# Writing the high half of each output row from ScalarE instead of VectorE, in an attention and two-stage MLP kernel

## The chip, the cores and the metric

The kernel runs on one core of a Trainium2 chip. Times are device microseconds (us) of one execution, from launch to end. Five engines work side by side, each on its own in-order queue: TensorE (PE: matmuls; PEld: its weight loads), VectorE (DVE), ScalarE (ACT), GpSimd (POOL) and SyncE (SP), the last of which issues most of the DMAs. Instructions of different engines wait for each other by semaphores.

## The reference

Three stages follow one another, all in float32:

```
scores = x @ state^T / 8;  a = softmax(scores);   xread = a @ state          # 8 x 8 heads, 512 rows, 32 states, 64 wide
scores2 = state @ x^T / 8; a2 = softmax(scores2); sread = a2 @ x
t = rows of [xread, sread], 4352 x 512
u = (sigmoid(t @ w_gate) * (t @ w_val)) @ w_out                              # 512 -> 1536 -> 512
e = argmax(u @ moe2_w_gate); p = softmax(u @ moe2_w_gate)[e]
out = p * (relu(u @ w1[e]) @ w2[e])                                          # 8 experts, 512 -> 1024 -> 512
```

The kernel does float32 products as three matmuls of float16 halves: every operand is scaled by a power of two and split into a high half (the value rounded to float16) and a low half (the scaled value minus the high half).

## The kernel before, in words

After a preparation, the function `token_block` runs for blocks b = 0 to 7, one for each batch of 512 tokens. A block has a gate phase and an output phase. In the gate phase `gate_val` is called for 12 feature chunks: matmuls L686 to L688, a sigmoid on ScalarE (L692), a product on VectorE (L694), the high half on ScalarE (L699) and the low half on GpSimd (L700). In the output phase `mlp_out` is called for four row tiles of 128 tokens: 36 matmuls (L744 to L746) sum into one PSUM buffer `po`. VectorE then takes the maximum of each row (L750), makes a power of two `s` of it in two tiny instructions (L142, L143), writes the high half of the scaled row as float16 into `xrow` (L755) and then the low half (L756). Two more row tiles, of the state rows, follow behind block 7: 34 row tiles in all. The rows are later sent by GpSimd to a table in DRAM, sorted by expert (`route`), and from about 780 us on the expert matmuls read them.

PSUM buffers of the kind `mm` number four. Gates, output tiles and the state weights share them.

Other work is woven into a block at marks. `mid()` is called twice in each gate chunk (marks 1 to 24) and three times in each output tile (marks 25 to 36: after the matmuls of feature chunks 3 and 7, and at the end of the tile, behind L756; the tile ends are marks 27, 30, 33 and 36). At a mark, fixed pieces are issued by number: the attention of the next block (`att_unit`, whose last piece, at marks 33 and 36, copies a result out of PSUM on ScalarE, L463), the state weights of the next block (`state_weights`, at marks 24, 26, ... 34: matmuls L489, high half on ScalarE L498, low half on VectorE L500), and the routing of this block (`route`: at mark 27 matmuls and a copy of the logits by ScalarE, L774; at mark 29 their transposes, L778). Behind these, `pump(bg)` takes one step of a background generator. From block 1 on this is `conv_experts`, which loads 64 chunks of expert weights and splits them, in three steps a chunk, one step a mark: (1) the high half on ScalarE and the low half on VectorE (L321, L322); (2) the bound of the next chunk, a sum of absolute values on ScalarE, two instructions on line L638; (3) the load of a later chunk, and the spread of the bound over the partitions by a tiny matmul (L202, reading the tile `em`), from which VectorE makes the scale. The pump runs at every output mark, and at the gate marks whose number is not a multiple of three.

The order of TensorE's instructions is as written (L960). The order on the other engines is made by a planner that simulates the program, gives precedence to what is written first, and keeps one kind of extra edge: under `tc.issue_after(ins)` the instructions of the block that run on the engine of `ins` are queued behind it. `mid()` opens such a block from block 1 on:

```
            for k in "AD":
                if k in last:
                    pins.enter_context(tc.issue_after(last[k].ins))
...
            with behind() if b else ExitStack():
                for f in todo.get(half[0], ()):
                    f()
```

`last["A"]` is an instruction of ScalarE and `last["D"]` one of VectorE. Before the change they are set by `gate_val` (L693, L694), by `state_weights` (L498, L500), and `last["D"]` also by `mlp_out` (L756).

Of the kernel before, what the change touches and what calls it, by code (L numbers as in the profile page):

```python
# [13 lines left out]
AF = mybir.ActivationFunctionType  # L14
ALU = mybir.AluOpType
# [11 lines left out]
def attention_moe_router_kernel(  # L27
# [24 lines left out]
    nc = tc.nc  # L52
    B, H, S, D = x.shape
    NS = state.shape[2]
    NT, DM = out.shape
# [77 lines left out]
    def tl(shape, dt=F32, name="t", bufs=None, pool=None):  # L133
        kw = {} if bufs is None else {"bufs": bufs}
        return (pool or tiny).tile(shape, dt, name=name, tag=name, **kw)

    def pow2_scale(m, k, nm, lim=40, inv=True, bufs=None, out=None, sh=0):

        n = m.shape[1]
        a = tl([P, n], I32, nm + "a")  # L140
        s = tl([P, n], I32, nm + "s", bufs) if out is None else out.bitcast(I32)
        nc.vector.tensor_scalar(a, m.bitcast(I32), EXPO, EXPO, ALU.bitwise_and, ALU.bitwise_xor)  # L142
        nc.vector.tensor_scalar(  # L143
            s, a, float((128 + lim) * ONE), float((k - 1) * ONE), ALU.min, ALU.add
        )
        if not inv:
            return s.bitcast(F32), None
        c = tl([P, n], I32, nm + "c", bufs)
        nc.vector.tensor_scalar(c, s, -1.0, float((254 - sh) * ONE), ALU.mult, ALU.add)
        return s.bitcast(F32), c.bitcast(F32)  # L150
# [42 lines left out]
    def mm_ps(shape):  # L193
        return mm_p.tile(shape, F32, name="mm", tag="mm")
# [22 lines left out]
    last = {}  # L217
# [520 lines left out]
    def mlp_out(t, j, acts, mid):  # L738

        po = mm_ps([P, DM])  # L740
        for fc, (h, lo) in enumerate(acts):
            hj, lj = h[:, j * P:(j + 1) * P], lo[:, j * P:(j + 1) * P]
            wh = wout[:, fc, 1] if t else ho[fc // 4][:, fc % 4]
            nc.tensor.matmul(po, hj, wh, start=(fc == 0), stop=False)  # L744
            nc.tensor.matmul(po, hj, wout[:, fc, 0], start=False, stop=False)  # L745
            nc.tensor.matmul(po, lj, wh, start=False, stop=(fc == NFC - 1))  # L746
            if fc in (3, 7):
                mid()
        m = tl([P, 1], name="xm")
        nc.vector.tensor_reduce(m, po, axis=AX.X, op=ALU.max, apply_absolute_value=True)  # L750
        r = rt[t // 4]
        s, _ = pow2_scale(m, 2, "xs", lim=80, inv=False, out=r["s"][:, j:j + 1])
        row = xrow[t % 4]
        pr = row[:, 0:DM].bitcast(F16)
        nc.vector.tensor_scalar(pr[:, 0:DM], po, s, None, ALU.mult)  # L755
        last["D"] = nc.vector.scalar_tensor_tensor(  # L756
            pr[:, DM:2 * DM], po, s, pr[:, 0:DM], op0=ALU.mult, op1=ALU.subtract
        )
        mid()
# [361 lines left out]
    def token_block(b):  # L1121
# [95 lines left out]
        for j in range(NJ):  # L1217
            mlp_out(NJ * b + j, j, acts, mid)
# [108 lines left out]
    for j in range(NST):  # L1327
        mlp_out(NXT + j, j, acts, lambda: next(tail, None) if j == 1 else None)
# [171 lines left out]
```

## Time and profile before

| | us |
|---|---|
| median of three runs | 1178.92 (1177.67 to 1181.25) |
| the profiled execution | 1176.91 |
| its span, from the first to the last instruction | 1175.2 |
| TensorE matmuls busy | 1077.7 (92%) |
| VectorE busy | 849.7 (72%) |
| ScalarE busy | 560.0 (48%) |
| GpSimd busy | 284.7 (24%) |
| L755, the instruction that is moved, 34 times | 25.5 |

The profile is of one execution. Busy time is the time in which an engine ran an instruction; the share is of the whole span, over stages with different limits. In the timeline a row gives start, duration, engine, line, operation, output and inputs, shapes and count; a bracket tells how long the engine had been idle before and what ended that. TensorE's clock has two levels, 1.2 and 2.4 GHz; a granted clock of 1.00 is the higher one all the time.

### The profile page before, as it was taken

The numbers are of one execution on the slowest core, as the hardware profiler recorded it, in microseconds if no ns is written. First come the engines' busy times: TensorE is split into PE (matmuls) and PEld (weight loads), VectorE is DVE, ScalarE is ACT, GpSimd is POOL, SyncE is SP. The second block draws the span as 40 slices with busy tenths as digits, with TensorE's granted clock in tenths as the row PEclk, the third lists the DMA queues.
The fourth block names the chain that finished last, engine by engine and source line by source line (L and its number), as shares of the span: only waits on it lengthen the run. The fifth ranks groups of instructions, "written<-read, shape, count | busy, mean of one in ns | idle before, by whom it ended". The sixth has DMA issues, their size and how long they took to land. (4 is left out here: it accounts for less than half of the span.)

```text
span 1175.2 us, 22595 instructions
## 1 busy us (share of the span) xinstructions
PE 1077.7 (92%) x8459; PEld 590.9 (50%) x8459; DVE 849.7 (72%) x2068; ACT 560.0 (48%) x970; POOL 284.7 (24%) x293
## 2 busy tenths in 40 slices
PE   3277689899999999998999999999999999999997
PEld 2122244444344444443444445866677666776664
DVE  7899966887887978878879756258666666665664
ACT  3676755757857768568577663311111111111111
POOL 1122211524415425134053250410000000000000
PEclk9978789999999999999999999999999999999999
DMA  7515492737657576476666451653222495989339
GB/s 259 193 58 163 113 178 61 221 103 226 183 160 227 148 204 203 113 202 193 162 210 169 143 196 55 207 182 129 57 56 56 144 358 124 281 288 363 60 103 280
DMA packets 187745, 200.66 MB, mean 171 GB/s; under 512 B 130159, under 2 KB 154735, under 8 KB 184304
## 3 DMA queue, kind: packets, MB, share of 16 engines
q1 hardware_dynamic: 172736, 147.51, 45.6%
q0 software_dynamic: 14896, 51.67, 11.5%
q8 instruction: 68, 1.11, 0.4%
q14 instruction: 45, 0.37, 0.1%
HBM read 217.40 MB, written 54.88 MB: 232 GB/s over the span
## 5 line engine op out<-in xcount | busy, mean ns | idle before, releaser
L935 ACT CAST acth<-v 128x256 f16<-128x256 f32 x148 | 60.1, 406 | 329.0 <-DVE v L934 306.0
L700 POOL TENSOR_TENSOR actl<-g,acth 128x512 f16<-128x512 f32 (+1 forms) x108 | 140.0, 1300 | 182.2 <-ACT acth L699 181.7
L688 PE MATMUL mm<-aT,M 128*128 128x512 f16 x384 | 149.6, 390 | 15.1 <-ACT M L510 15.1
L745 PE MATMUL mm<-wout,acth 128*128 128x512 f16 x408 | 155.7, 382 | 0.2 <-DVE wout L322 0.2
L686 PE MATMUL mm<-aT,M 128*128 128x512 f16 x384 | 149.1, 388 | 5.1 <-ACT g L692 4.4
L744 PE MATMUL mm<-wout,acth 128*128 128x512 f16 x396 | 150.3, 380 | 1.0 <-ACT g L692 1.0
L746 PE MATMUL mm<-wout,actl 128*128 128x512 f16 x396 | 150.1, 379 | 0.0
L687 PE MATMUL mm<-aT,M 128*128 128x512 f16 x384 | 149.2, 389 | 0.0
L920 PEld LDWEIGHTS <-wgv 128*128 128x128 f16 x1184 | 115.8, 98 | 18.6 <-DMA wgv<-w_d 1.3
L920 PE MATMUL mm<-big,wgv 128*128 128x256 f16 x736 | 123.9, 273 | 0.0
L923 PE MATMUL mm<-big,wgv 128*128 128x128 f16 x736 | 122.7, 219 | 0.0
L949 POOL DMA_INDIRECT out_dram<-g,meta x37 | 35.9, 971 | 343.3 <-DVE g L946 295.4
L923 PEld LDWEIGHTS <-wgv 128*128 128x128 f16 x1184 | 115.8, 98 | 4.0
L933 DVE TENSOR_REDUCE v<-mm 128x256 f32<-128x512 f32 x148 | 101.5, 686 | 18.5 <-PE mm L923 17.4
L936 DVE TENSOR_TENSOR actl<-v,acth 128x256 f16<-128x256 f32 x148 | 62.9, 425 | 68.7 <-ACT acth L935 68.3
L322 DVE SCALAR_TENSOR_TENSOR out<-big,inv,out 128x1024 f16<-128x1024 f32 x64 | 82.9, 1295 | 36.1 <-ACT out L321 36.1
L694 DVE SCALAR_TENSOR_TENSOR g<-mm,g 128x512 f32<-128x512 f32 (+1 forms) x108 | 71.0, 657 | 44.8 <-PE mm L688 23.5
L321 ACT ACTIVATE out<-big,inv 128x1024 f16<-128x1024 f32 x64 | 73.3, 1146 | 52.7 <-DVE inv L143 45.6
L692 ACT ACTIVATE g<-mm,sgf 128x512 f32<-128x512 f32 (+1 forms) x108 | 71.4, 661 | 34.6 <-POOL actl L700 23.8
L699 ACT CAST acth<-g 128x512 f16<-128x512 f32 (+1 forms) x108 | 63.5, 590 | 38.9 <-DVE g L694 38.8
L671 POOL DMA_DIRECT2D w_d<-out x63 | 35.6, 564 | 189.2 <-DVE out L322 138.1
L920 PE MATMUL mm<-out,wgv 128*128 128x256 f16 x448 | 75.4, 273 | 0.8 <-DMA wgv<-w_d 0.8
(324 smaller groups left out, 2133.6 us busy)
## 6 DMA issues: line engine op xcount, KB each, us to landing
wgv<-w_d SPq DMA_DIRECT2D x56, 2048.0 KB
wout<-w_d SPq DMA_DIRECT2D x18, 2048.0 KB
big<-in_moe_w_dram SPq DMA_DIRECT2D x64, 512.0 KB
w_d<-out POOLq DMA_DIRECT2D x64, 512.0 KB, 5.1
xb<-in_x_dram SPq DMA_DIRECT2D x60, 128.0 KB
wgv<-in_moe_w_gate_dram SPq DMA_DIRECT2D x3, 1024.0 KB
wgv<-in_moe_w_val_dram SPq DMA_DIRECT2D x3, 1024.0 KB
wout<-in_moe_w_gate_dram SPq DMA_DIRECT2D x3, 1024.0 KB
```

The lines of the kernel that those rows point to most:

```text
L321: nc.scalar.activation(h16, v, AF.Copy, scale=s)
L322: nc.vector.scalar_tensor_tensor(l16, v, s, h16, op0=ALU.mult, op1=ALU.subtract)
L686: nc.tensor.matmul(ps[k], w[0], v[0], start=(i == 0), stop=False)
L687: nc.tensor.matmul(ps[k], w[0], v[1], start=False, stop=False)
L688: nc.tensor.matmul(ps[k], w[1], v[0], start=False, stop=(i == len(parts) - 1))
L700: last["P"] = nc.gpsimd.tensor_tensor(lo, g, h, op=ALU.subtract)
L744: nc.tensor.matmul(po, hj, wh, start=(fc == 0), stop=False)
L745: nc.tensor.matmul(po, hj, wout[:, fc, 0], start=False, stop=False)
L746: nc.tensor.matmul(po, lj, wh, start=False, stop=(fc == NFC - 1))
L920: nc.tensor.matmul(ph[:, i], w1s[:, pr, c, 0, f], t[:, :, c], start=(c == 0), stop=False)
L923: nc.tensor.matmul(ph[:, i, 1], w1s[:, pr, c, 1, f], t[:, 0, c], start=False, stop=(c == NDC - 1),)
L933: nc.vector.tensor_reduce(v, ph.rearrange("p i l q -> p i q l"), axis=AX.X, op=ALU.add)
```

## The change

In `mlp_out` the high half of the row tile is written by a ScalarE Copy with the scale `s` in place of the VectorE multiply. The Copy is also stored as `last["A"]`. The maximum, the scale and the low half stay with VectorE, and the low half reads the high half as before.

```
--- before.py
+++ after.py
@@ -752,7 +752,7 @@
         s, _ = pow2_scale(m, 2, "xs", lim=80, inv=False, out=r["s"][:, j:j + 1])
         row = xrow[t % 4]
         pr = row[:, 0:DM].bitcast(F16)
-        nc.vector.tensor_scalar(pr[:, 0:DM], po, s, None, ALU.mult)
+        last["A"] = nc.scalar.activation(pr[:, 0:DM], po, AF.Copy, scale=s)
         last["D"] = nc.vector.scalar_tensor_tensor(
             pr[:, DM:2 * DM], po, s, pr[:, 0:DM], op0=ALU.mult, op1=ALU.subtract
         )
```

## Rows read from the trace of the kernel before

**Rows 1.** The page, part 2: TensorE's busy tenths in 40 slices of 29.4 us.
```profile
PE   3277689899999999998999999999999999999997
```

**Rows 2.** Windows: length; busy PE, PEld, DVE, ACT, POOL; clock; DMA share; GB/s.
```profile
390.00:429.00 39.00, 38.80 (x333) 17.10 (x332) 33.75 (x87) 24.22 (x41) 9.46 (x10) 1.00 0.63 153
429.00:467.00 38.00, 36.05 (x228) 16.70 (x232) 31.86 (x83) 31.35 (x50) 22.75 (x21) 1.00 0.72 222
300.00:304.00 4.00, 4.00 (x13) 1.40 (x10) 3.48 (x7) 3.53 (x5) 1.44 (x2) 0.57 0.85 212
```

**Rows 3.** Waits of PE, 157 to 1175 us: total us, times, longest.
```profile
PE at L202 <- ACT junk L638: 6.6, 5, 2.4
...
PE mm L489 <- DVE M L500: 0.4, 2, 0.2
```

**Rows 4.** Groups of DVE: what, shapes, count; busy us, mean ns; idle us before.
```profile
L756 DVE SCALAR_TENSOR_TENSOR xrow<-mm,f,xrow 128x512 f16<-128x512 f32 x34 | 25.5, 751 | 1.1
L755 DVE TENSOR_SCALAR xrow<-mm,f 128x512 f16<-128x512 f32 x34 | 25.5, 750 | 1.0
```

**Rows 5.** Timeline of DVE, first output tile of block 3.
```profile
401.88 1.29 DVE L500 SCALAR_TENSOR_TENSOR M<-mm,M 128x512 f16<-128x512 f32 x2
...
403.09 0.68 DVE L750 TENSOR_REDUCE xm<-mm 128x1 f32<-128x512 f32 x1
...
403.99 0.15 DVE L143 TENSOR_SCALAR f<-xsa 128x1 int32<-128x1 int32 x1
...
404.18 0.75 DVE L755 TENSOR_SCALAR xrow<-mm,f 128x512 f16<-128x512 f32 x1
404.96 0.75 DVE L756 SCALAR_TENSOR_TENSOR xrow<-mm,f,xrow 128x512 f16<-128x512 f32 x1
```

**Rows 6.** Groups of ACT, a per-row scale at 128x512.
```profile
L692 ACT ACTIVATE g<-mm,sgf 128x512 f32<-128x512 f32 (+1 forms) x108 | 71.4, 661 | 34.6 <-POOL actl L700 23.8 <-PE mm L688 9.8 <-PE at L202 0.9
...
L321 ACT ACTIVATE big<-wout,osc 128x512 f16<-128x512 f32 x12 | 7.5, 711 | 2.0 <-DVE osc L603 2.0
```

**Rows 7.** Timeline of ACT, 401 to 407 us.
```profile
401.26 1.08 ACT L498 ACTIVATE M<-mm 128x512 f16<-128x512 f32 x2
402.22 1.06 ACT L638 ACTIVATE junk<-big 128x1024 fp8e5<-128x1024 f32 x1
...
403.26 0.58 ACT L774 COPY ls<-at 128x512 f32<-128x512 f32 x1
```

**Rows 8.** Timeline of PE, block 3: output phase, then the next gate.
```profile
403.99 0.23 PE L202 MATMUL at<-identb,em 128*128 128x128 bf16 x1
...
406.65 0.60 PE L778 MATMUL at<-identf,ls 128*128 128x128 f32 x4
...
413.14 0.22 PE L202 MATMUL at<-identb,em 128*128 128x128 bf16 x1
...
423.56 0.22 PE L202 MATMUL at<-identb,em 128*128 128x128 bf16 x1
...
430.78 0.22 PE L202 MATMUL at<-identb,em 128*128 128x128 bf16 x1
```

**Rows 9.** Timeline of ACT, 410 to 434 us.
```profile
410.68 1.08 ACT L498 ACTIVATE M<-mm 128x512 f16<-128x512 f32 x2 [2.73 <-PE mm L489]
...
425.47 0.20 ACT L638 ACTIVATION_READ_ACCUMULATOR junk<-big 128x1 f32 x1
...
429.69 0.63 ACT L463 ACTIVATE x1s<-at,sc 64x64 f32<-64x64 f32 x2 [2.43 <-PE at L454]
```

**Rows 10.** Timeline of DVE, second and last output tile of block 3.
```profile
410.86 0.15 DVE L143 TENSOR_SCALAR f<-xsa 128x1 int32<-128x1 int32 x1
...
428.99 0.69 DVE L750 TENSOR_REDUCE xm<-mm 128x1 f32<-128x512 f32 x1 [0.41 <-PE mm L746]
...
429.90 0.15 DVE L143 TENSOR_SCALAR f<-xsa 128x1 int32<-128x1 int32 x1
```

**Rows 11.** Timeline of PE, 299 to 300.4 us.
```profile
299.80 0.23 PE L202 MATMUL at<-identb,em 128*128 128x128 bf16 x1 [2.42 <-ACT junk L638]
```

More of the change, by code (lines that the diff above doesn't have):

```diff
@@ L754, in mlp_out @@
         pr = row[:, 0:DM].bitcast(F16)
-        nc.vector.tensor_scalar(pr[:, 0:DM], po, s, None, ALU.mult)
+        last["A"] = nc.scalar.activation(pr[:, 0:DM], po, AF.Copy, scale=s)
         last["D"] = nc.vector.scalar_tensor_tensor(
```

## The prediction

> **What bounds the kernel now.** I read the slices of the page first [rows 1]: from the seventh slice on TensorE stands at 8 or 9 tenths to the end. It is the bound, and its order is written out by hand. So the question about any edit on the other engines is whether it makes TensorE wait longer or less. The stages [rows 2] say how little there is to win: in the output phase of block 3 (390 to 429 us) TensorE is busy 38.80 of 39 us, and in the gate phase behind it 36.05 of 38. In the same two stretches VectorE is busy 33.75 and 31.86 us, ScalarE 24.22 and 31.35. So the output phase is where ScalarE has room and VectorE has little.
>
> The waits of TensorE from 157 us on [rows 3] name the two kinds that matter here. The longest sum is 6.6 us in 5 waits of L202, the tiny matmul that spreads the bound of an expert chunk, for L638, the ScalarE pass that computes this bound. The L489 matmuls, which need a PSUM buffer back from VectorE, lose 0.4 us. No wait at all is charged to L755 or L756. So taking L755 off VectorE frees nothing that TensorE is seen to wait for, and a later L638 is what hurts it.
>
> **The change, part by part.** VectorE loses 34 instructions of 750 ns [rows 4], 25.5 us. On the path that sets the end I value this at zero: the 0.4 us of L489 [rows 3] end with L500, VectorE's low half of the state weights, and in block 3 that L500 stands ahead of the tile's maximum in VectorE's queue (401.88 against 403.09 [rows 5]), so it would come no sooner. The cover of the rest is TensorE's own work of about 9 us per tile; a tile's PSUM buffer is given back by L756, which comes no sooner either, as the next sum shows.
>
> ScalarE gains 34 passes over 128x512 from PSUM with a per-row scale. No such Copy is in the trace. The nearest row is the sigmoid, same shape, same source, per-row scale: 661 ns; the other bound is the 711 ns of a scaled Copy of that size from SBUF [rows 6]. I take 0.66 us. The low half cannot start before it, so the chain of a tile goes from 0.79 us (start of L755 at 404.18 [rows 5] to start of L756 at 404.96) to about 0.04 + 0.66 + 0.02 = 0.72 us if ScalarE is free: even. If no other VectorE work is put between, VectorE idles for what it was busy before.
> The Trainium skill ("ScalarE: Activation LUTs", Rules for kernel authors) says a multiply belongs on VectorE, not on ScalarE. Rows 4 and 6 disagree for this shape, 750 against 661 to 711 ns. The same page (What ACT_TABLE_LOAD costs) gives 186 ns + 0.833 ns an element and 93 ns for a scale read per row, an estimate of 706 ns: by it each stall below would be some 0.05 us longer.
>
> Now what is moved. The assignment to last["A"] is the part with a price. In blocks 1 and later, everything that is written out inside a mark is pinned, on ScalarE, behind the last instruction stored there. Before, that was the high half of the latest state weights (L498) or a sigmoid; VectorE's pin was already this tile's L756. After, at the mark that closes a tile, it is this tile's high half, and that needs the tile's maximum and scale from VectorE. So three kinds of ScalarE work wait for it: L638, L774 (copy of the router logits) and L463. The trace shows that they ran ahead of it: in block 3 L638 runs at 402.22 directly behind the L498 pair of 401.26, L774 at 403.26 [rows 7], while VectorE starts the tile's maximum only at 403.09 and has the scale at 403.99 + 0.15 = 404.14 [rows 5]. That L638 is one that belongs to the mark closing the tile; only the old pin let it run 2 us before the tile's scale was there.
>
> Which marks hold an L638 that TensorE soon wants? The conversion of expert weights takes three steps a chunk (scale and split; bound; spread), one per mark, at 16 of the 24 gate marks and all 12 output marks: 28 steps a block, which is 1 mod 3. So the cycle shifts by one each block and returns every third. Block 3 has the spread (L202) behind the state weights of mark 28, at 403.99, then at marks 31, 34 and at mark 1 of the next block [rows 8]: so its bounds sit at marks 27, 30, 33 and 36, exactly the four tile ends. Block 6 is the same. Blocks 1, 4, 7 and 2, 5 have the bounds one or two marks later. Block 0 pins nothing.
>
> The sum for block 3, with successive ScalarE instructions overlapping 0.1 us as in [rows 7], in the order in which they are written:
> - Mark 27: high half 404.18 to 404.84, L774 (0.58) to 405.33, L638 with its accumulator read (1.06 [rows 7] + 0.20 [rows 9] - 0.1) to 406.39. TensorE wants it at 403.99: a wait of 2.4 us. With L638 ahead of L774 it is 1.9.
> - Mark 30: scale at 410.86 + 0.15 [rows 10], high half 411.06 to 411.72, then the L498 pair that ran at 410.68 before [rows 9] (1.08) to 412.70, L638 to 413.76; wanted at 413.14: 0.6 us, or nothing if L638 goes ahead of L498. I take 0.3.
> - Mark 33: the spread at 423.56 [rows 8] comes 4.1 us behind the start of the maximum (419.46); the chain from maximum to L638 takes 3.4 us, as at mark 36: nothing.
> - Mark 36: scale at 430.05 [rows 10], high half to 430.75, L463 pair (0.63) to 431.3, L638 to 432.35. Before, this L638 was done at 425.47 + 0.20 [rows 9]. Wanted at 430.78: 1.6 us, or 1.05 if L638 goes first.
> That is 4.3 us in block 3 and the same in block 6: 8.6 us, with ends of 5.9 (2 x 2.95) and 9.2 (2 x 4.6). TensorE's order is fixed, so a wait of L202 holds up everything behind it: the output matmuls of the next tile, and at mark 1 the second half of the first gate.
>
> The rest is small. L774 is late by up to 5 us in other blocks too, but its transposes (L778) come at 406.65 in block 3 [rows 8], 2.5 us behind the scale, and high half plus copy need 1.2: covered; if other ScalarE work of more than 1.3 us got between, the excess would show. In blocks 2 and 5 a split and a bound at marks 27 and 28 queue behind the high half and just meet their spread: 0 to 0.2 us each. Register waits, DMAs and their queues are not touched: no DMA is issued by the moved instruction. In the expert stage after 780 us nothing changes.
>
> The profiled execution took 1176.91 us, 1.7 us over its span, and stands 2.0 us under the median of 1178.92. So 1176.9 + 8.6 = 1185.5 in that execution, and 1178.9 + 8.6 = 1187.5 beside the median.
>
> **Rivals.** About 0.3% (3.5 us) either way is what a measurement here tells from no change.
> - *The pins cost nothing* (15%): the planner puts VectorE's maximum earlier, or the waits of 2 us are given back in the next gate phase, where TensorE idles 1.95 us anyway [rows 2]. For it: ScalarE idles for much of the output phase. Against it: the maximum is late because VectorE works off older work (L500 at 401.88 [rows 5]), which keeps its precedence. It gives 1178.9, at most 3.5 to either side.
> - *VectorE's relief decides* (11%), the other side: the 25.5 us come off an engine that is 87% busy in the output phase, so the gate phase begins with less backlog, and waits behind a late ScalarE or VectorE shrink. The 6.6 us of L202 [rows 3] would be halved and one drop of the clock would go: after the 2.42 us wait at 299.80 [rows 11] the granted clock over 300 to 304 us is 0.57 [rows 2], 4 x 0.43 = 1.7 us of the full clock lost. 3.3 + 1.7 = 5.0: 1173.9. It decides if less than 1 us of new wait arises at the four tile ends of blocks 3 and 6. Against it: at the last tile of the block VectorE is idle for 0.41 us until the tile's last matmul at 428.99 [rows 10], so it enters the gate phase without a backlog that could shrink.
> - *The new waits also drop the clock*: the mark 27 waits are as long as the one at 299.80. Twice 1.7 us on top gives 1190.8. One row of such a drop does not say that every wait of this length brings one, so it stands in the forecast's own range and not in its value.
>
> **How the numbers follow.** Forecast, new waits of L202 for L638: 74%, 1187.5, own range 1183 to 1191 (5.9 less some given back; 9.2 with a clock drop or two). No effect 15%, relief 11%. The range for 8 in 10 takes in part of the no-effect case: 1178 to 1192. Slower 0.74, same 0.15, faster 0.11.
>
> **What would show it.** In the profile after: L202 waiting for L638 grows from 6.6 us to about 15, with two waits of about 2 us behind the state weights of mark 28 in blocks 3 and 6 and two of 1 to 1.6 us at the first mark of the blocks after them; L774 and L638 stand behind the new Copy on ScalarE at tile ends. VectorE's busy time falls by about 25 us and ScalarE's rises by about 22, with no table load added. I am wrong if the sum of TensorE's waits does not grow, if L638 still runs ahead of the Copy at mark 27, or if the waits grow and the time does not.

## The result, and the profile after

The change makes the kernel slower: 1194.35 us against 1178.93 us (medians of six runs each), ratio 1.0142 with a 95% interval of 1.011 to 1.0174. That is 15.4 us by the medians and 16.7 by the ratio. The direction was predicted; the time lies 6.9 us above the forecast and 2.35 us above the range. The profiled execution took 1195.55 us, 18.6 more than the one of before.

First the page: busy time by engine, then the two lines that the change touches or disturbs (busy us, mean ns, idle before).

```profile
PE 1081.8 (91%) x8459; PEld 591.6 (50%) x8459; DVE 837.9 (70%) x2034; ACT 580.2 (49%) x1004; POOL 287.0 (24%) x293
...
L322 DVE SCALAR_TENSOR_TENSOR out<-big,inv,out 128x1024 f16<-128x1024 f32 x64 | 90.9, 1421 | 38.4 <-ACT out L321 38.0
...
L755 ACT ACTIVATE xrow<-mm,f 128x512 f16<-128x512 f32 x34 | 23.4, 687 | 115.2 <-DVE f L143 115.2
```

The Copy takes 687 ns, between the 661 and 711 of [rows 6]. ScalarE gains 20.2 us (predicted about 22). VectorE loses 11.8 us and not 25.5: L322, the low half of the expert weights, takes 1421 ns where it took 1295 before, which alone gives 8 us back. (That is no property of the move: with the Copy and no pin, the first experiment below, VectorE loses 26.3 us.) ScalarE's mean idle time in front of the Copy, 115.2 / 34 = 3.4 us, ends each time with L143: it is the scale, from VectorE, that ScalarE now waits for.

The waits of TensorE from 157 to 1190 us answer to [rows 3] (us in total, times, longest):

```profile
PE at L202 <- ACT junk L638: 19.6, 13, 2.9
PE mm L686 <- ACT g L692: 7.1, 4, 4.1
```

L202 waiting for L638 has grown from 6.6 us to 19.6. Here is ScalarE at the end of block 2, at the first tile end of block 3 (answering to [rows 7]) and around the last one:

```profile
353.07 0.69 ACT L755 ACTIVATE xrow<-mm,f 128x512 f16<-128x512 f32 x1 [3.75 <-DVE f L143]
...
354.30 1.15 ACT L321 ACTIVATE out<-big,inv 128x1024 f16<-128x1024 f32 x1
355.35 1.04 ACT L638 ACTIVATE junk<-big 128x1024 fp8e5<-128x1024 f32 x1
...
356.50 1.28 ACT L692 ACT_TABLE_LOAD   x1
357.80 0.69 ACT L692 ACTIVATE g<-mm,sgf 128x512 f32<-128x512 f32 x1
...
406.65 0.69 ACT L755 ACTIVATE xrow<-mm,f 128x512 f16<-128x512 f32 x1 [1.84 <-DVE f L143]
407.24 1.05 ACT L638 ACTIVATE junk<-big 128x1024 fp8e5<-128x1024 f32 x1
...
408.28 0.57 ACT L774 COPY ls<-at 128x512 f32<-128x512 f32 x1
...
425.00 0.69 ACT L755 ACTIVATE xrow<-mm,f 128x512 f16<-128x512 f32 x1 [2.69 <-DVE f L143]
...
427.28 1.13 ACT L333 ACTIVATE xn<-xb,uxs 128x1024 f16<-128x1024 f32 x1
...
432.42 1.15 ACT L321 ACTIVATE out<-big,inv 128x1024 f16<-128x1024 f32 x1 [2.68 <-DVE inv L143]
...
435.90 0.69 ACT L755 ACTIVATE xrow<-mm,f 128x512 f16<-128x512 f32 x1 [2.33 <-DVE f L143]
436.48 0.62 ACT L463 ACTIVATE x1s<-at,sc 64x64 f32<-64x64 f32 x2
437.13 1.06 ACT L638 ACTIVATE junk<-big 128x1024 fp8e5<-128x1024 f32 x1
```

At 406.65 ScalarE has been idle for 1.84 us when the scale comes; L638 stood behind the Copy, and TensorE was waiting for it by the time it ran. At the end of block 2 a Copy, a split and a bound stand in front of the table load and the first sigmoid of the next gate phase. In the kernel before, the same stretch of block 2 read:

```profile
350.35 1.15 ACT L321 ACTIVATE out<-big,inv 128x1024 f16<-128x1024 f32 x1 [1.95 <-DVE inv L143]
352.42 0.63 ACT L463 ACTIVATE x1s<-at,sc 64x64 f32<-64x64 f32 x2 [0.92 <-PE at L454]
353.76 1.28 ACT L692 ACT_TABLE_LOAD   x1 [0.71 <-PE mm L688]
355.06 0.69 ACT L692 ACTIVATE g<-mm,sgf 128x512 f32<-128x512 f32 x1
```

TensorE ran the same 8459 matmuls in the same order, so each can be set beside itself. These are waits of after at the places that the prediction named and in the gate phases of blocks 3, 5 and 7, from TensorE's timeline (the bracket is the wait):

```profile
356.54 0.23 PE L202 MATMUL at<-identb,em 128*128 128x128 bf16 x1 [0.98 <-ACT junk L638]
...
408.43 0.23 PE L202 MATMUL at<-identb,em 128*128 128x128 bf16 x1 [1.89 <-ACT junk L638]
...
438.33 0.23 PE L202 MATMUL at<-identb,em 128*128 128x128 bf16 x1 [2.94 <-ACT junk L638]
...
540.15 0.58 PE L686 MATMUL mm<-aT,M 128*128 128x512 f16 x1 [4.14 <-ACT g L692]
...
652.15 0.23 PE L202 MATMUL at<-identb,em 128*128 128x128 bf16 x1 [1.78 <-ACT junk L638]
...
680.68 0.23 PE L202 MATMUL at<-identb,em 128*128 128x128 bf16 x1 [1.58 <-ACT junk L638]
...
694.69 0.23 PE L202 MATMUL at<-identb,em 128*128 128x128 bf16 x1 [2.07 <-ACT junk L638]
```

Subtracting start times of the same matmul in the two traces, and looking where the difference grows, gives these steps. The gate phases are, by the times of before, 352 to 390, 431 to 467, 507 to 548, 587 to 624 and 664.6 to 696 us; the second and the last start behind mark 1.

| place | step, us |
|---|---|
| behind mark 28, blocks 3 and 6 (408.43, 652.15) | 1.96 and 1.85 |
| mark 1 of blocks 4 and 7 (438.33, 680.68) | 3.11 and 1.74 |
| the four together | 8.66 |
| gate phase of block 3, 4, 5, 6, 7 | 2.2, 0.9, 1.6, 2.6, 3.6 |
| those five together | 11.0 |
| given back elsewhere | -1.0 |
| in all | 18.6 |

So the places that the prediction named cost what it said, 8.66 us against 8.6, and more than as much again was lost in this execution where it looked for nothing. Not all of that is the pin's, as the traces of the experiments show.

### The profile page after: what moved, and what is told of

It reads as the page before. It is cut to its first block, busy times and chain, and to the rows that moved or that the text cites. A ratio compares the mean times of both kernels' runs of the same rounds, so it can differ in the third digit from the quotient of the medians.

```text
span 1193.8 us, 22610 instructions
## 1 busy us (share of the span) xinstructions
PE 1081.8 (91%) x8459; PEld 591.6 (50%) x8459; DVE 837.9 (70%) x2034; ACT 580.2 (49%) x1004; POOL 287.0 (24%) x293
## 5 line engine op out<-in xcount | busy, mean ns | idle before, releaser
L700 POOL TENSOR_TENSOR actl<-g,acth 128x512 f16<-128x512 f32 (+1 forms) x108 | 139.7, 1299 | 184.4 <-ACT acth L699 183.9
L686 PE MATMUL mm<-aT,M 128*128 128x512 f16 x384 | 150.7, 393 | 8.3 <-ACT g L692 7.1
L322 DVE SCALAR_TENSOR_TENSOR out<-big,inv,out 128x1024 f16<-128x1024 f32 x64 | 90.9, 1421 | 38.4 <-ACT out L321 38.0
L933 DVE TENSOR_REDUCE v<-mm 128x256 f32<-128x512 f32 x148 | 101.5, 686 | 18.6 <-PE mm L923 18.4
L692 ACT ACTIVATE g<-mm,sgf 128x512 f32<-128x512 f32 (+1 forms) x108 | 71.3, 661 | 38.5 <-POOL actl L700 28.3
L321 ACT ACTIVATE out<-big,inv 128x1024 f16<-128x1024 f32 x64 | 73.2, 1143 | 15.2 <-DVE inv L143 14.2
L755 ACT ACTIVATE xrow<-mm,f 128x512 f16<-128x512 f32 x34 | 23.4, 687 | 115.2 <-DVE f L143 115.2
```

What stands on the lines that cost most here:

```text
L321: nc.scalar.activation(h16, v, AF.Copy, scale=s)
L322: nc.vector.scalar_tensor_tensor(l16, v, s, h16, op0=ALU.mult, op1=ALU.subtract)
L686: nc.tensor.matmul(ps[k], w[0], v[0], start=(i == 0), stop=False)
L700: last["P"] = nc.gpsimd.tensor_tensor(lo, g, h, op=ALU.subtract)
L933: nc.vector.tensor_reduce(v, ph.rearrange("p i l q -> p i q l"), axis=AX.X, op=ALU.add)
```

## The experiments

All ratios are to the kernel before on the same chip, with 95% intervals; 0.3% is 3.5 us. Edits are shown against the changed kernel unless said otherwise.

**The two halves of the edit.** First the Copy alone: it is no longer stored as the pin.

```
-        last["A"] = nc.scalar.activation(pr[:, 0:DM], po, AF.Copy, scale=s)
+        nc.scalar.activation(pr[:, 0:DM], po, AF.Copy, scale=s)
```

> ScalarE writes the high half as in the change, but the Copy is not stored as last["A"]. Theory P (the pin delays ScalarE's bound L638 and split L321 at tile ends, and TensorE waits for them): back to the kernel before, 1176 to 1183 us; L202 waits for L638 fall from 19.6 to about 7 us. Rival M (the move itself costs: 23.4 us more on ScalarE, the longer chain to the low half, GpSimd and DMA order): 1190 us or more, with the waits still near 15 us.

Measured: 1.003 [1.0003, 1.0057]. Then the pin alone: VectorE writes the high half as before, and a ScalarE copy of the 128x1 scale is the pin.

```
-        last["A"] = nc.scalar.activation(pr[:, 0:DM], po, AF.Copy, scale=s)
+        nc.vector.tensor_scalar(pr[:, 0:DM], po, s, None, ALU.mult)
+        last["A"] = nc.scalar.copy(tl([P, 1], name="pin"), s)
```

> VectorE keeps the high half; a ScalarE copy of the 128x1 scale is added in each tile and stored as last["A"], so the pin stands without the move. Theory P: 1188 to 1196 us, a little under the change because the tiny copy ends some 0.5 us sooner than the Copy. Rival M: 1177 to 1182 us.

Measured: 1.0105 [1.007, 1.0139]. At the four places of the table TensorE makes steps of 1.48, 1.37, 2.15 and 1.26 us in this trace, and of 0.00 with the Copy alone. The same row of TensorE's waits, first of the Copy alone, then of the pin alone:

```profile
PE at L202 <- ACT junk L638: 6.6, 5, 2.4
```

```profile
PE at L202 <- ACT junk L638: 15.6, 12, 2.4
```

The sum of the first is that of [rows 3], but it is made up of other waits: one of 2.08 us in the gate phase of block 7 has come, and the one of 2.42 us in that of block 5 has gone. The pin brings most of the waits and of the time; the Copy brings about 0.3%, with no more waiting for L638 in all.

**Which pinned work?** In the next two kernels the tile's Copy pins only a part of what a mark issues: in the first the fixed pieces (attention, state weights, routing), in the second the background steps (split, bound, spread). Their core, with `last["T"]` the Copy, `at_mark` a copy of `last`, and the letters given to `behind` the pins that it opens (the second has the two strings the other way round):

```
-            with behind() if b else ExitStack():
+            at_mark = dict(last)
+            with behind("ATD", at_mark) if b else ExitStack():
                 for f in todo.get(half[0], ()):
                     f()
+            with behind("AD", at_mark) if b else ExitStack():
                 if half[0] > 12 if b == 0 else half[0] > GV or half[0] % 3:
                     pump(bg)
```

> The change with its pin for the fixed pieces of a mark only (state weights, L774, L463, the attention); the step of the expert conversion (L638, L321) is pinned as before the change. Theory P, in the form that L638 and L321 are what costs: 1177 to 1184 us. Rival T (L774, L463 and the attention behind the Copy are what costs): 1190 us or more.

Measured: 1.0029 [1.0005, 1.0052], the level of the Copy without any pin.

> The reverse of the kernel in which only the fixed pieces saw the new pin: here the fixed pieces of a mark (attention, state weights, routing) are pinned on ScalarE as before the change, and only the background steps of the conversion (split, bound, spread) stand behind the Copy. If the late bound and split carry the cost, the ratio stays near that of the change, 1.011 to 1.015, and the waits of L202 for L638 sum to 15 to 20 us as after. If the late logits copy or the late attention copy carry a part, the ratio falls below 1.009 and the waits below 12 us.

Measured: 1.0094 [1.0077, 1.0111]. The waits, in the same order:

```profile
PE at L202 <- ACT junk L638: 8.7, 8, 2.4
```

```profile
PE at L202 <- ACT junk L638: 13.5, 10, 2.5
```

Late fixed pieces alone cost nothing that can be told. The late bound and split alone cost 0.6% over the Copy (7.5 us), and the two together 1.1% (13.2 us). The figure fell between the two cases that were expected; the waits, at 13.5, too. The trace shows one way in which they meet. With only the background steps pinned, the step at mark 1 of block 4 is 1.58 us and not 3.11. In the changed kernel L333, a fixed piece, runs at 427.28 behind the Copy of mark 33 at 425.00 (above). It ran at 420.81 before, so it is 6.5 us later, where TensorE is 4.6 us later (435.39 against 430.78, below). VectorE's half of it, L337, then stands in front of the reduction that makes the scale for the split. VectorE in the changed kernel:

```profile
428.45 1.67 DVE L337 SCALAR_TENSOR_TENSOR xn<-xb,uxs,xn 128x256 f16<-128x256 f32 x4 [1.98 <-ACT xn L333]
...
430.31 0.28 DVE L209 TENSOR_REDUCE er<-at 128x1 f32<-128x128 f32 x1
...
433.60 1.28 DVE L322 SCALAR_TENSOR_TENSOR out<-big,inv,out 128x1024 f16<-128x1024 f32 x1 [1.07 <-ACT out L321]
434.80 0.68 DVE L750 TENSOR_REDUCE xm<-mm 128x1 f32<-128x512 f32 x1
```

L337, L209, L321 and L322 follow one another, and the maximum of the last tile, L750, comes behind L322. It starts 0.59 us ahead of the point at which TensorE wants L202 (438.33 - 2.94 = 435.39); before it was 1.79 us (428.99 [rows 10], 430.78 [rows 8]). With only the background steps pinned, L333 runs ahead of that Copy, at 423.11, and L750 starts 1.45 us ahead (432.01; TensorE wants L202 at 434.88 - 1.42 = 433.46). There L463 also runs ahead of the Copy of mark 36, and not between it and the bound:

```profile
432.21 0.63 ACT L463 ACTIVATE x1s<-at,sc 64x64 f32<-64x64 f32 x2 [1.44 <-PE at L454]
433.11 0.69 ACT L755 ACTIVATE xrow<-mm,f 128x512 f16<-128x512 f32 x1 [0.27 <-DVE f L143]
433.69 1.05 ACT L638 ACTIVATE junk<-big 128x1024 fp8e5<-128x1024 f32 x1
```

The wait is 1.42 us in that kernel and 2.94 in the changed one. Of the 1.5 us between them 0.86 is the later maximum (1.45 - 0.59), and 0.65 is L463: L638 starts 0.58 us behind the start of the Copy there, and 1.23 here.

**Which tile?** The pin at the last tile of a block only, then at the first only.

```
-        last["A"] = nc.scalar.activation(pr[:, 0:DM], po, AF.Copy, scale=s)
+        hi = nc.scalar.activation(pr[:, 0:DM], po, AF.Copy, scale=s)
+        last["A"] = hi if j == 3 else last["A"]      # second kernel: j == 0
```

> The change, but the Copy is stored as last["A"] in the last tile of a block only. If the waits at the first mark of a block and the late start of ScalarE in the gate phase are most of the cost (in the two profiles: shift of 3.1 and 1.7 us at mark 1 of blocks 4 and 7, and 11 us inside gate phases), 1189 to 1194 us. If the first tile (shift of 2.0 and 1.9 us at mark 28) and the middle ones carry it, under 1185 us.

Measured: 1.0116 [1.005, 1.0182].

> The Copy stays, and it is stored as the pin only at the first row tile of a block (marks 25 to 27 behind it see it until the next state weights replace it). In the trace this should bring back the wait behind mark 28 of blocks 3 and 6 (about 1.96 and 1.85 us, 3.8 together) and leave the first marks of blocks 4 and 7 and the starts of the gate phases behind blocks 2 and 5 as with the Copy without a pin. Theory 1, the waits alone cost what they last: ratio to before 1.003 + 3.8/1178.9 = 1.006. Theory 2, such a wait also drops TensorE's clock (3.4 us of half clock behind it were seen in block 3, so 1.7 us each): 1.003 + 7.2/1178.9 = 1.009. Rival, the cost belongs to the last tile alone (the pin there gave 1.0116): 1.003.

Measured: 1.0063 [1.0046, 1.008], the figure of theory 1. The two steps behind mark 28 are back, 1.96 and 1.85 us, and the kernel costs 0.33% (3.9 us) over the Copy alone. With the intervals of both kernels that is 3.9 us with 3.8 to either side, so theory 2 is less likely by this number and not excluded. The last tile is worth 0.86% (10 us, with 8 to either side), of which the four-place table above holds 4.85.

**Which blocks?** The same edit with `t // 4 in (3, 6)`, `(2, 5)` or `(1, 4)` in place of `j == 3`.

> The change, but the Copy is stored as last["A"] in blocks 3 and 6 only, the two blocks that the prediction's sum was made of. Prediction as it stands: this carries the cost, 8 to 9 us over the kernel before. Second theory (the sum of these blocks is right, and a late ScalarE at the start of a gate phase costs as much again in other blocks): 9 to 12 us over, with L202 waits of about 2 us at mark 28 and 1.5 to 3 us at mark 1 of blocks 4 and 7, and the other two kernels carry the rest.

Measured: 1.0135 [1.0085, 1.0186].

> The Copy is stored as last["A"] in blocks 2 and 5 only. Prediction as it stands: 0 to 0.4 us over the kernel before and its Copy, so like the Copy without a pin (ratio 1.003). Second theory: the split L321 of mark 36 and the bound L638 of mark 1 stand behind the last tile's Copy and hold the table load and the first sigmoid of the next gate phase some 2.7 us; from the two profiles (2.5 us before block 3's output phase, 2.6 us before block 6's) about 5 us over the Copy without a pin.

Measured: 1.0044 [1.0016, 1.0071].

> The Copy is stored as last["A"] in blocks 1 and 4 only. Both theories: no L638 or L321 of these blocks is near its use at a tile end, so 0 to 2 us over the Copy without a pin. If each pin costs by itself, whatever work is behind it, 4 to 5 us.

Measured: 1.0032 [0.9999, 1.0066].

Over the Copy alone that is 12.4, 1.7 and 0.2 us, each with 5 to 7 us to either side, and 12.4 + 1.7 + 0.2 + 3.5 for the Copy is 17.8, against 16.7 for the whole change: the parts add up within that noise. Blocks 3 and 6 carry it, as the counting of steps modulo three said. In that kernel TensorE's steps at the four places are again 1.96, 3.11, 1.85 and 1.74; they are 0.00 with the pin in blocks 2 and 5 or 1 and 4.

**Which steps in the gate phases are the pin's?** The same subtraction against before, us:

| gate phase of block | 3 | 4 | 5 | 6 | 7 |
|---|---|---|---|---|---|
| the change | 2.2 | 0.9 | 1.6 | 2.6 | 3.6 |
| the Copy without a pin | 0.6 | -1.0 | 0.2 | 0.4 | 2.8 |
| pin in blocks 1 and 4 | 1.1 | -1.0 | 0.0 | 0.5 | 3.7 |
| pin in blocks 2 and 5 | 2.4 | 0.2 | 0.3 | 3.1 | 1.1 |
| pin at the last tile | 4.3 | 1.1 | 3.9 | 2.5 | 3.6 |

The steps of blocks 3 and 6 come where the pin stands at the end of the block before. Timed, the pin in blocks 2 and 5 is only 1.7 us above the Copy alone, with 4.5 to either side. The step of block 7 is mostly not the pin's: it is there with the Copy alone and with the pin in blocks that are far from it. Its wait of 2.07 us for L638 (694.69 above) begins with ScalarE waiting for a buffer from GpSimd. So does a wait of 2.08 us for L638 with the Copy alone (690.17), at the spread of the next chunk. ScalarE in the changed kernel, then with the Copy alone:

```profile
692.91 0.69 ACT L692 ACTIVATE g<-mm,sgf 128x512 f32<-128x512 f32 x1 [3.60 <-POOL actl L700]
```

```profile
688.39 0.69 ACT L692 ACTIVATE g<-mm,sgf 128x512 f32<-128x512 f32 x1 [2.37 <-POOL actl L700]
```

In the gate phases of blocks 3, 4 and 6 of the changed kernel one L322 each (362.56, 448.31, 607.67) also took 3.7 to 3.9 us in place of 1.28, while GpSimd issued an indirect DMA and ran two L700. The first:

```profile
362.56 3.77 DVE L322 SCALAR_TENSOR_TENSOR out<-big,inv,out 128x1024 f16<-128x1024 f32 x1 [1.38 <-ACT out L321]
```

With the pin in blocks 2 and 5 the same L322 of blocks 3 and 6 took 3.9 us; with the Copy alone none took over 2.3. So part of what these phases lose may come by VectorE and not by a late ScalarE alone; no kernel here separates the two.

**TensorE's clock behind the waits.** The windows give length, busy times by engine, granted clock, DMA share and GB/s. The pin in blocks 3 and 6, behind the 1.89 us wait at mark 28 (here at 404.39):

```profile
404.00:408.00 4.00, 3.61 (x11) 1.41 (x12) 2.69 (x8) 2.94 (x6) 0.00 (x0) 0.57 0.68 126
```

The pin at the first tile, behind waits of 1.90 us (410.93) and 1.78 us (648.30):

```profile
410.90:414.90 4.00, 3.97 (x12) 1.50 (x13) 1.92 (x6) 3.50 (x6) 0.00 (x0) 0.57 0.58 102
648.30:652.30 4.00, 4.00 (x22) 2.15 (x23) 2.62 (x8) 3.48 (x6) 0.00 (x0) 1.00 1.06 241
```

The changed kernel behind its waits of 1.89, 2.94 and 4.14 us:

```profile
408.40:412.40 4.00, 3.97 (x22) 2.12 (x23) 2.96 (x7) 2.59 (x4) 0.00 (x0) 1.00 0.56 100
438.30:442.30 4.00, 3.97 (x26) 1.85 (x27) 2.63 (x8) 3.99 (x5) 1.02 (x1) 1.00 0.67 255
540.20:544.20 4.00, 4.00 (x10) 1.38 (x10) 3.19 (x11) 2.94 (x5) 3.04 (x4) 0.50 1.14 232
```

The same wait at mark 28 is followed by a granted clock of 0.57, which is mostly the lower level, in two kernels and by full clock in a third. A drop is real, and 4 x 0.43 = 1.7 us each, but a place does not own one: it cannot be added up per wait. For the profiled executions TensorE's busy time over the same 8459 matmuls sizes it: 1077.7 us before, 1081.8 after, 1083.8 with the Copy alone. By this a slower clock is about 4 of the 18.6 us in these executions, and it is no more than with the Copy alone.

**Giving the bound more time.** In the code before, the spread of a bound is issued one mark later, with the split of its chunk. This is the generator of the expert weights; the diff is to the kernel before:

```
+            if n:
+                scale(n)
             pair(v, o[:, :, 0], o[:, :, 1], sc.pop(n))
             yield
             bound(n + 1)
...
             load(n + 3)
-            scale(n + 1)
             yield
```

> The kernel before (high half on VectorE, no new pin), with the spread of a chunk's bound written one mark later, together with the split of the same chunk, so that two marks lie between L638 and the L202 that needs it. If the waits of TensorE for L638 (6.6 us) cost their sum and nothing takes their place: 1169 to 1174 us. If the split L321 then waits on ScalarE's queue for the scale and delays the sigmoids behind it: 1178 us or more.

Measured: 1.005 [1.0025, 1.0075], a small loss. L202 no longer waits for L638 at all (6.6 us before); other waits took its place, those of L686 for the sigmoid (8.4 us, 4.4 before) and of L365 for the transfer of `xT` (5.9 us, 0.5 before) above all. The same edit beside the change, with and without its pin:

> The change as it is, with its pin, and beside it the spread of a bound over the partitions issued one mark later (in the step that splits, as in the kernel in which this was done to the code before). A bound that is held behind the Copy at a tile end then has a whole mark more, about 3 us, before TensorE wants it. If the late bound (L638) in front of TensorE's spread (L202) is what the change costs, the waits of L202 for L638 fall from 19.6 us to under 4 and the ratio to before falls to that of the two parts without it, 1.003 for the Copy to 1.008 (Copy 1.003 plus the late spread itself 1.005). If the late fixed pieces or a late VectorE carry the cost, it stays at 1.011 or above and the waits turn up at other lines.

Measured: 1.0106 [1.0076, 1.0137].

> The Copy on ScalarE without the pin, and the spread one mark later: the level to hold the run beside it against. Both parts alone were 1.003 and 1.005; if they add, 1.008. If the two ease each other (the late spread takes away the 6.6 us of L202 waiting for L638 that the Copy alone leaves), it comes out below 1.003, and below 0.997 it would be faster than both kernels.

Measured: 1.0075 [1.0047, 1.0104]: the two parts add up (1.008) and do not ease each other. The first missed what was expected, 1.003 to 1.008. Read against the second it still tells: the pin costs 0.3% here (3.7 us) where it cost 1.1% (13.2), each with about 5 us to either side. Its waits of L202 for L638 are 4.0 us, and the longest of them, 2.75 us at 439.08, is the old one at the block's end. ScalarE there:

```profile
434.79 1.28 ACT L693 ACT_TABLE_LOAD   x1 [0.85 <-PE mm L689]
436.08 0.69 ACT L693 ACTIVATE g<-mm,sgf 128x512 f32<-128x512 f32 x1
436.67 0.68 ACT L756 ACTIVATE xrow<-mm,f 128x512 f16<-128x512 f32 x1
...
437.88 1.06 ACT L638 ACTIVATE junk<-big 128x1024 fp8e5<-128x1024 f32 x1
```

Lines behind the edit are one higher here (the Copy is L756, the sigmoid L693). Given a mark more, the planner put the table load and the sigmoid in front of the Copy, and the bound is late again. No kernel here beats the one before.

## Why the prediction went wrong, point by point

- *TensorE bounds the kernel, and a later L638 is what hurts.* Right. The pin alone makes 1.0105, the pin for everything but the conversion steps nothing over the Copy alone, and TensorE's steps at the four places are there only in kernels that pin these steps there.
- *Only blocks 3 and 6 have their bounds at the tile ends.* Right as to where most of the cost lies: 12.4 us there (5.6 to 19.1), 0.2 in blocks 1 and 4 (-4.8 to 5.3).
- *Mark 27, 2.4 us or 1.9 with L638 ahead of L774.* The second branch came: 1.89 and 1.78 us of waiting. *Mark 30, 0.3; mark 33, nothing*: TensorE's times make no step there.
- *Mark 36, 1.6 us.* In block 6 right (1.58). In block 3, where the prediction worked it out, it is 2.94, because the maximum itself had become late through L333 and L337. The prediction kept VectorE's queue as it was before and delayed only ScalarE's.
- *The sum, 8.6 us.* These four places give 8.66, which is partly luck: the high figure of one mark makes up for the low figures of the others.
- *The step that failed* is "The rest is small", with "in blocks 2 and 5 ... 0 to 0.2 us each", and the value of nothing that the sum gave to the Copy itself. The step looked at marks 27 and 28 of blocks 2 and 5 and not at the last: there the split and the bound stand behind the Copy and in front of the table load, and the first sigmoid runs at 357.80 instead of 355.06, 2.7 us late, where TensorE is 1.3 us late. It gave no price to what a gate phase loses when ScalarE enters it behind: 2.2 and 2.6 us in blocks 3 and 6 of the profile, where the Copy alone loses 0.6 and 0.4. In timed runs the 16.7 us are 3.5 for the Copy without a pin [0.4, 6.7] and 13.2 for the pin, of which 4.5 is beyond the four places, with about 5 to either side. Either term alone would have left the time in the range or at its edge; the Copy's is the one that timing tells from nothing.
- *VectorE's relief is worth nothing, and the Copy's chain is even.* The chain is right where ScalarE is free, as the prediction said: in the changed kernel VectorE idles 0.76 us in front of L756 at most tiles, 21.6 us in all, where 0.72 was predicted and L755 took 0.75 before. With the Copy alone, which other ScalarE work may precede, it idles up to 2.18 us. The rule of the Trainium skill ("ScalarE: Activation LUTs", Rules for kernel authors) that a multiply belongs on VectorE does not hold for this instruction by itself: 687 ns against 750. That the Copy costs nothing did not hold: 1.003 with an interval just clear of 1.
- *The new waits also drop the clock* (the end of the range; its 1190.8 should be 1187.5 + 3.4 = 1190.9). In the changed kernel's profile the mark 27 waits did not. The drop there stands behind the 4.14 us wait at 540.15, and that one is not new: at the same matmul TensorE waited before, and longer with the Copy alone.

```profile
529.39 0.38 PE L686 MATMUL mm<-aT,M 128*128 128x512 f16 x1 [2.04 <-ACT g L692]
```

```profile
537.04 0.38 PE L686 MATMUL mm<-aT,M 128*128 128x512 f16 x1 [3.87 <-ACT g L692]
```

In the changed kernel and with the Copy alone the wait of 2.42 us that followed in the kernel before, at 536.53, is gone in return. The wait at 540.15 begins on GpSimd, whose next indirect DMA waited for the one before it and held L700 behind it, and so the buffer of the next sigmoid. GpSimd, then ScalarE's idle time of 3.86 us:

```profile
535.42 1.28 POOL L847 DMA_INDIRECT rows_d<-xrow,rri  x1 [4.22 <-DMA rows_d<-xrow,rri]
...
537.28 3.21 POOL L700 TENSOR_TENSOR actl<-g,acth 128x512 f16<-128x512 f32 x2
```

```profile
539.41 0.69 ACT L692 ACTIVATE g<-mm,sgf 128x512 f32<-128x512 f32 x1 [3.86 <-POOL actl L700]
```

- *TensorE stands at 8 or 9 tenths to the end.* Its last slice in [rows 1] is at 7; nothing hangs on it.

What stays open: why the Copy without a pin costs 0.3%. Its profile has a 4.2 us wait of L686 for L692 and a lower clock behind it, at 224.39, but the kernel in which only the fixed pieces are pinned has no such wait (2.5 us is its longest) and the same ratio. What the two have in common is the wait of 2.1 us in the gate phase of block 7, where they lose 2.8 and 1.4 us. But the trace of the pin alone, whose high half is VectorE's, loses 2.8 there too, so the one trace of the kernel before may be the odd one. How much of the steps in the gate phases is there in every execution is open too, since each trace shows one; and block 7's own pin was never tried alone.

## What to carry to other kernels

Before an instruction is made the point behind which other work is queued, list everything that is queued there at every mark, not only what has a visible wait today: a producer with 2 us of slack becomes the bound when its engine is held for 2 us. Then follow that engine into the next stage: work that arrives in a burst behind a late pin sits in front of the next stage's first instruction, and a second engine that reads its output is shifted as well. Before a wait in the trace after is put down to the change, look for the same instruction in the trace before and in the kernel with half of the edit: two of the longest waits here were not the pin's. When the engine is moved for one instruction only, leave the pin on what is early, and time the move alone before trusting the busy time that it takes off.

## What the runs showed that was not expected

A Copy of 128x512 from PSUM to float16 with a scale per row took 687 ns on ScalarE, against 750 on VectorE for the same values. Taking 25.5 us of instructions off VectorE lowered its busy time by 11.8 us only. The mean of L322 went from 1295 to 1421 ns through a few of the 64: 57 took 1.29 us or less, and three, beside work of GpSimd, 3.7 to 3.9. With the Copy alone the mean is 1338 ns and the busy time fell by 26.3 us. No experiment here isolated why the three were so long. The same wait of 1.9 us in front of the same matmul was followed by a granted clock of 0.57 in some traces and of 1.00 in others.
